# An Exp table loaded early, two converted matrices and one row maximum moved in the start of a three-stage attention kernel

## Chip, cores and metric

One NeuronCore of a Trainium2 chip runs the whole program. The metric is the device time of one execution in microseconds (us); the time shown for a kernel is the median of its runs.

## What is computed

Three stages follow each other for a batch of 4 with 576 positions. The first is decayed causal attention with 8 heads of 64, the second mixes the positions with a low-rank product and adds a feed-forward layer, the third is a mixture of four attention experts. The change touches only the first stage and the load of `U` and `V`, which the second stage starts with:

```python
log_f = np.log(np.clip(f, 0.0001, 1.0))
cum = np.cumsum(log_f, axis=-1)
scores = where(causal, -1e9, scale * q @ k.T + cum[:, :, :, None] - cum[:, :, None, :])
scores = scores - np.max(scores, axis=-1, keepdims=True)
attn = np.exp(scores); attn /= attn.sum(-1, keepdims=True) + 1e-9
x = attn @ v                      # first stage
h = x.transpose(0, 2, 1) @ U @ V  # start of the second stage
u = x + h.transpose(0, 2, 1)
```

## The kernel before

The first stage works through 32 heads in 16 pairs. For a head (0 is the first) the steps are these.

- `row_max` (lines 150 to 187) finds the maximum of each row of scores. It multiplies the queries by the keys into two PSUM tiles, `ua` (line 154, two products) and `ub` (line 163, four products), and VectorE adds the mask and reduces them: one instruction at line 158 for `ua`, four at line 176 for `ub`. TensorE then transposes the five columns of maxima (`mt`, line 181), VectorE scales them into `mr` (line 183), and two small DMAs on the SP queue (lines 185 and 186) put them into row 66 of the queries `qa`. `row_max` is a generator: `one(...)` runs it to its next `yield`. With `apart` true there is a stop between `ua` and `ub`.
- `scores` (lines 189 to 227) multiplies again, now with row 66 and with low parts, in two halves. The first half is a PSUM tile of five products, the second one of twelve (line 212). ScalarE takes the exponential of a half (line 221) and rounds it to float16 (`ph`, line 222); VectorE subtracts for the low part `pl` (line 223).
- `weighted_values`, `row_scales` and `normalise` multiply by the values and divide.

`ua`, `ub` and the score halves all come from one PSUM pool with two buffers (tag `s2` of pool `ps2`). A tile waits until what stood in its buffer has been read.

Before the first head, lines 446 to 458 take the logarithm of the decays on ScalarE (line 451), sum it and store it; `load_pair`, `split_high` and `split_low` (lines 482 to 522) load two heads, round them on ScalarE (lines 499 to 502), subtract on GpSimd (lines 519 to 522) and copy parts between partitions by DMAs on SP (lines 513 to 518).

`load_mix` (lines 584 to 599) loads `U` in one DMA and `V` in two (SP), as 64-bit words whose halves `narrow` (lines 302 to 310) makes into float32: a shift on VectorE (line 307), a scaled copy on ScalarE (line 308), and two more on VectorE (309, 310). For `U` three GpSimd copies follow (line 590), for each half of `V` a ScalarE copy and a GpSimd subtraction (lines 598, 599). The raw words share two buffers (tag `wraw`) and the results one (tag `wst`), so the second half of `V` can be loaded only when `U` is narrowed. `U` and `V` are first read by `mix(0)`, in head 3.

What sets the order. `first_batch` (lines 645 to 678) runs the first eight heads, and its TensorE instructions are issued in the order in which they are written. Everything before it, and the queues of VectorE, ScalarE, GpSimd and SP, are ordered by a planner that takes what it expects to be ready first. `tc.issue_after(ins)` makes the instructions of its block that go to `ins`'s queue stand behind `ins`; `cur["last"]` is the latest DMA of line 186, so in the kernel before the loads of `U` and `V` stand behind the row-maxima DMA of head 0, since line 630 comes before `first_batch`:

```python
    drain(maxima(0, 0))
    m_first = maxima(0, 1)
    one(m_first)               # head 1: ua and ub, ahead of first_batch
...
    with tc.issue_after(cur["last"].ins):
        load_mix()
```

In `first_batch` head `h` issues: first half of its scores, `ua` of head `h + 2`, second half of its scores, the transposed maxima of head `h + 1`, `ub` of head `h + 2`, and the weighted values of head `h - 1`. Between these stand the scales of the values and the mixing.

Of the kernel before, what the change touches and what calls it, by code (L numbers as in the profile page):

```python
# [8 lines left out]
F32 = mybir.dt.float32  # L9
# [4 lines left out]
AF = mybir.ActivationFunctionType  # L14
# [3 lines left out]
P = 128  # L18
# [35 lines left out]
def f32(ap):  # L54
    return ap.bitcast(F32)
# [3 lines left out]
def kernel(  # L59
# [13 lines left out]
    nc = tc.nc  # L73
# [4 lines left out]
    def pool(name, bufs=1, side="left", space=None):  # L78
        kw = {} if space is None else {"space": space}
        if space is None:  # L80
            kw["side"] = side
            kw["reuse_waits"] = "tile"
        return tc.alloc_tile_pool(name=name, bufs=bufs, **kw)
# [6 lines left out]
    small = pool("small", 4)  # L90
# [45 lines left out]
    cur = {}  # L136
# [5 lines left out]
    def drain(gen):  # L142

        while True:
            try:
                next(gen)
            except StopIteration as end:
                return end.value
# [80 lines left out]
    def weighted_values(ph, pl, vh, vl):  # L229

        av = ps1.tile([P, NT, 65], F32, name="av")
        for it in range(NT):
            order = list(range(it + 1)) if it < NT - 1 else [0, 4, 1, 2, 3]
            for jt in order:
                c = J_OFF[jt] + (it - jt) * P
                m = 64 if jt == 4 else P
                k = 64 if jt == 4 else P
                first, last = jt == order[0], jt == order[-1]
                nc.tensor.matmul(av[0:m, it, :], ph[0:k, c:c + m], vh[0:k, jt, :],  # L239
                                 start=first, stop=False)  # L240
                nc.tensor.matmul(av[0:m, it, 0:64], ph[0:k, c:c + m], vl[0:k, jt, :],  # L241
                                 start=False, stop=False)
                nc.tensor.matmul(av[0:m, it, :], pl[0:k, c:c + m], vh[0:k, jt, :],  # L243
                                 start=False, stop=last)
        return av
# [28 lines left out]
    def row_scales(av, rs, extra=None):  # L274

        den = small.tile([P, NT], F32, name="den")
        nc.vector.tensor_scalar(den[:], av[:, :, 64:65].rearrange("p t o -> p (t o)"),
                                1.0e-9 * PSCALE * VEXP, rs[:, 0:1], OP.add, OP.mult)
        rn = small.tile([P, NT], F32, name="rn")
        nc.vector.reciprocal(rn[:], den[:])  # L280
        if extra is not None:
            nc.vector.tensor_tensor(rn[:], rn[:], extra, OP.mult)
        return rn

    def normalise(dst, av, rn):
        nc.vector.tensor_tensor(dst, av[:, :, 0:64], rn[:].unsqueeze(2).to_broadcast([P, NT, D]),  # L286
                                OP.mult)
# [7 lines left out]
    def next_mx():  # L295
        counter[0] += 1
        return mxs[counter[0] % 4]
# [4 lines left out]
    def narrow(wt, raw, n, p0=0, p1=P):  # L302


        lo, hi = raw[p0:p1, :, 0], raw[p0:p1, :, 1]
        wi = wt.bitcast(I32)
        nc.vector.tensor_scalar(wi, lo, 29, None, OP.logical_shift_right)
        nc.scalar.activation(f32(lo), f32(hi), AF.Copy, scale=2.0 ** -112)
        nc.vector.scalar_tensor_tensor(wi, lo, 3, wi, OP.logical_shift_left, OP.bitwise_or)
        nc.vector.scalar_tensor_tensor(wi, hi, -2147483648, wi, OP.bitwise_and, OP.bitwise_or)  # L310
# [135 lines left out]
    fr = pre.tile([B * H, S], F32, name="fr")  # L446
# [2 lines left out]
    nc.vector.memset(ones[:], 1.0)  # L449
    nc.vector.tensor_scalar(fr[:], fr[:], 1.0e-4, 1.0, OP.max, OP.min)  # L450
    nc.scalar.activation(fr[:], fr[:], AF.Ln)
    cum = pre.tile([B * H, S], F32, name="cum")
    nc.vector.tensor_tensor_scan(cum[:], ones[:], fr[:], 0.0, OP.mult, OP.add)
    chl = pre.tile([B * H, 2, S], F32R, name="chl")
# [24 lines left out]
    def pair_heads(p):  # L479
        return heads[2 * (p % 2)], heads[2 * (p % 2) + 1]  # L480

    def load_pair(p):
        if p >= NPAIR:
            return
        sin = sins[p % 2 if p < NP else 0]
        qkt = sin.tile([P, 2, S], F32, name="qkt")
        nc.sync.dma_start(qkt[:], qk[p // NP, p % NP])
        vr = sin.tile([P, 2, NT, D], F32, name="vr")
        nc.sync.dma_start(vr[:], v[p // NP, p % NP])
        st_in[p] = (qkt, vr)  # L490
# [33 lines left out]
    def values(p):  # L524
        if p >= NPAIR:
            return
        vr = st_in[p][1]
        st_rs[p] = yield from value_scale(vr[:])
        value_parts(vr[:], st_rs[p], *vhs[p % 2])

    def maxima(p, j, apart=False):
        if p < NPAIR:
            yield from row_max(pair_heads(p)[j], next_mx(), apart)

    def one(gen):

        next(gen, None)

    def attend(p, j):
        vh, vl = vhs[p % 2]  # L540
        ph, pl = st_p[p, j]
        av = weighted_values(ph, pl, vh[:, j], vl[:, j])
        rn = row_scales(av, st_rs[p])
        normalise(xs[p][:, :, j * D:j * D + D], av, rn)
# [27 lines left out]
    split_low(0)  # L572
    drain(values(0))
    drain(maxima(0, 0))
    m_first = maxima(0, 1)
    one(m_first)
    load_pair(1)
    split_high(1)
    split_low(1)
# [4 lines left out]
    def load_mix():  # L584
        ur = stage.tile([P, 2 * NT * R], I32, name="ur", tag="wraw")
        nc.sync.dma_start(ur[:], u_in)
        u1 = stage.tile([P, NT * R], F32, name="u1", tag="wst", bufs=1)
        narrow(u1[:], ur[:].rearrange("p (n two) -> p n two", two=2), NT * R)
        for r in range(3):
            nc.gpsimd.tensor_copy(ut[:, :, r * R:r * R + R],  # L590
                                  u1[:].rearrange("p (t r) -> p t r", t=NT))
        for c in range(NC):
            cs = slice(c * HC, c * HC + HC)
            vraw = stage.tile([3 * R, 2 * HC], I32, name="vraw", tag="wraw")
            nc.sync.dma_start(vraw[:], v_in[:, 2 * c * HC:2 * c * HC + 2 * HC])
            vst = stage.tile([3 * R, HC], F32, name="vst", tag="wst", bufs=1)
            narrow(vst[:], vraw[:].rearrange("p (n two) -> p n two", two=2), HC, 0, 3 * R)
            nc.scalar.copy(vs[:, cs], vst[:])
            nc.gpsimd.tensor_tensor(vs[64:96, cs], vst[64:96, :], f32(vs[64:96, cs]), OP.subtract)
# [6 lines left out]
    def load_weights(wp, q):  # L606
        gen = load_quarter_steps(wp, q)
        W[q] = next(gen)
        behind.append(gen)
# [17 lines left out]

    load_weights(wx_pool, 0)
    load_weights(wy_pool, 1)
    with tc.issue_after(cur["last"].ins):  # L630
        load_mix()
    def weights_after(p):
        if p < len(WRATE):
            with tc.issue_after(cur["last"].ins):
                more_weights(WRATE[p])

    def next_inputs(p):
        load_pair(p)
        split_high(p)
        split_low(p)  # L640

    def pair_scores(p, j):
        st_p[p, j] = yield from scores(pair_heads(p)[j])

    def first_batch(m_next):

        mixing = vals = iter(())
        for h in range(2 * NP):  # L650
            p, j = divmod(h, 2)
            sc = pair_scores(p, j)
            m_last, m_next = m_next, maxima(p + 1, j, True)
            one(sc)
            one(m_next)
            if j == 0:
                xs[p] = sx.tile([P, NT, P], F32, name="x", bufs=2)
                vals = values(p + 1)
                one(vals)
            one(sc)  # L660
            one(m_last)
            if j == 1:
                next_inputs(p + 2)
            one(m_next)
            if j == 1:
                one(vals)
            if h > 0:
                attend(*divmod(h - 1, 2))
            if j == 0:
                one(vals)  # L670
                one(mixing)
            elif p > 0:
                mixing = mix(p - 1)
                one(mixing)
            if j == 1:
                weights_after(p)
        one(mixing)
        return m_next
# [64 lines left out]
    with tc.manual_schedule(engines={mybir.EngineType.PE}):  # L743
        later_batches(first_batch(m_first))
# [369 lines left out]
```

## Time and profile before

| | |
|---|---|
| median of 3 runs | 938.31 us (938.24 to 939.66) |
| span of the profiled execution | 939.0 us (the page gives no other time for it) |
| TensorE busy | 847.3 us, 90% |
| VectorE, ScalarE, GpSimd busy | 60%, 44%, 31% |
| mean granted TensorE clock | 0.954 |

The page's second part cuts the span into 40 slices of 23.5 us and gives the busy share of each engine in tenths, and under PEclk the granted clock of TensorE in tenths of full speed. The timeline gives each instruction with its start and its length; brackets show how long its engine had been idle and what ended that. The chain follows the work that ended last back to the start. SPq is the queue on which SP issues DMAs: its rows are the issue, not the transfer.

### The profile page before, as it was taken

The numbers are of one execution on the slowest core, as the hardware profiler recorded it, in microseconds if no ns is written. First come the engines' busy times: TensorE is split into PE (matmuls) and PEld (weight loads), VectorE is DVE, ScalarE is ACT, GpSimd is POOL, SyncE is SP. The second block draws the span as 40 slices with busy tenths as digits, with TensorE's granted clock in tenths as the row PEclk, the third lists the DMA queues.
The fourth block names the chain that finished last, engine by engine and source line by source line (L and its number), as shares of the span: only waits on it lengthen the run. The fifth ranks groups of instructions, "written<-read, shape, count | busy, mean of one in ns | idle before, by whom it ended". The sixth has DMA issues, their size and how long they took to land.

```text
span 939.0 us, 18998 instructions
## 1 busy us (share of the span) xinstructions
PE 847.3 (90%) x7480; PEld 792.6 (84%) x7480; DVE 562.3 (60%) x1468; ACT 415.3 (44%) x808; POOL 294.1 (31%) x262
## 2 busy tenths in 40 slices
PE   2886878999899989989998999999999897989897
PEld 2775767888899989989998999999999797978675
DVE  6798588787576657632256652222225778786653
ACT  4675546564445463332233342222113464644553
POOL 8545354353423333012135433323014131210100
PEclk9998567999999999999999999999999998989998
DMA  6345545353433341103178753424114130311222
GB/s 190 106 108 163 141 149 166 112 146 114 126 109 86 111 136 47 39 15 114 53 267 262 233 185 113 152 74 121 37 29 124 39 90 17 91 29 27 70 85 69
DMA packets 68777, 101.94 MB, mean 109 GB/s; under 512 B 6608, under 2 KB 49424, under 8 KB 68688
## 3 DMA queue, kind: packets, MB, share of 16 engines
q1 hardware_dynamic: 64416, 92.47, 33.4%
q10 hardware_dynamic: 4272, 8.26, 2.5%
q8 instruction: 59, 0.97, 0.4%
q14 instruction: 30, 0.25, 0.1%
HBM read 60.33 MB, written 22.56 MB: 88 GB/s over the span
## 4 chain that ended last, share of the span: by engine, by line
PE 70%; DVE 14%; DMA 6%; ACT 5%; issue 3%; POOL 1%; SPq 1%; POOLq 0%; ACTq 0%; DVEq 0%
PE cps L385 19%; PE hps L370 19%; PE sc L212 8%; PE pq L849 4%; PE po L935 3%; PE pv L892 3%; PE av L239 3%; DVE pl L223 2%; DMA ust<-udram 2%; PE ub L169 2%; DVE ub L176 2%; PE gp L552 2%; PE av L243 2%; PE av L241 2%; PE ua L156 1%
## 5 line engine op out<-in xcount | busy, mean ns | idle before, releaser
L385 PE MATMUL cps<-hh,w2h 128*128 128x288 f32 x512 | 155.4, 304 | 6.8 <-DVE yc L387 3.8
L223 DVE TENSOR_TENSOR pl<-pf,ph 128x576 f16<-128x576 f32 x144 | 121.6, 847 | 54.4 <-ACT ph L222 54.2
L385 PE MATMUL cps<-hh,w2l 128*128 128x288 f32 x512 | 152.2, 297 | 1.0 <-POOL w2l L345 1.0
L370 PE MATMUL hps<-uh,w1h 128*128 128x288 f32 x512 | 145.2, 305 | 6.7 <-ACT uh L355 6.7
L385 PE MATMUL cps<-hl,w2h 128*128 128x288 f32 x512 | 151.2, 295 | 0.0
L370 PE MATMUL hps<-uh,w1l 128*128 128x288 f32 x512 | 141.9, 299 | 0.0
L375 DVE SCALAR_TENSOR_TENSOR hl<-hps,hh 128x288 fp32r<-128x288 f32 x128 | 58.2, 455 | 127.3 <-ACT hh L374 127.1
L374 ACT ACTIVATE hh<-hps 128x288 fp32r<-128x288 f32 x128 | 52.3, 409 | 168.6 <-PE hps L370 168.4
L221 ACT ACTIVATE pf<-sc 128x576 f32<-128x576 f32 x144 | 83.6, 612 | 52.3 <-PE sc L212 48.6
L385 PEld LDWEIGHTS cps<-hh,w2h 128*128 128x128 f32 x512 | 97.1, 190 | 8.3 <-DVE yc L387 4.5
L370 PEld LDWEIGHTS hps<-uh,w1h 128*128 128x128 f32 x512 | 97.9, 191 | 7.2 <-ACT uh L355 7.2
L370 PEld LDWEIGHTS hps<-uh,w1l 128*128 128x128 f32 x512 | 98.0, 191 | 0.0
L385 PEld LDWEIGHTS cps<-hh,w2l 128*128 128x128 f32 x512 | 96.9, 189 | 1.2 <-POOL w2l L345 1.2
L385 PEld LDWEIGHTS cps<-hl,w2h 128*128 128x128 f32 x512 | 96.9, 189 | 0.0
L370 PE MATMUL hps<-ul,w1h 128*128 128x288 f32 x512 | 89.6, 297 | 3.2 <-POOL ul L356 3.2
L212 PE MATMUL sc<-qa,ka 67*128 67x288 f32 (+4 forms) x288 | 79.1, 334 | 14.6 <-DMA qa<-mr 5.5
L222 ACT CAST ph<-pf 128x576 f16<-128x576 f32 x144 | 88.7, 638 | 1.6
L239 PE MATMUL av<-vh,ph 128*128 128x65 f16 x720 | 86.4, 202 | 1.5 <-DVE x L286 1.5
L176 DVE CUSTOM_DVE_ANT_0 ub<-ub,maskm 128x448 f32<-128x448 f32 x192 | 81.4, 424 | 7.2 <-PE ub L169 6.0
L241 PE MATMUL av<-vl,ph 128*128 128x64 f16 x720 | 85.1, 198 | 0.0
L243 PE MATMUL av<-vh,pl 128*128 128x65 f16 x720 | 84.8, 198 | 0.0
L356 POOL TENSOR_TENSOR ul<-ust,uh 128x1152 fp32r<-128x1152 f32 x22 | 58.8, 2671 | 80.9 <-ACT uh L355 80.9
(160 smaller groups left out, 1984.9 us busy)
## 6 DMA issues: line engine op xcount, KB each, us to landing
raw<-in_w_dram SPq DMA_DIRECT2D x32, 512.0 KB
ust<-udram SPq DMA_DIRECT2D x22, 576.0 KB
qkt<-in_qk_dram SPq DMA_DIRECT2D x16, 576.0 KB
yc<-ydram SPq DMA_DIRECT2D x14, 576.0 KB
ydram<-yc SPq DMA_DIRECT2D x14, 576.0 KB
vr<-in_v_dram SPq DMA_DIRECT2D x16, 320.0 KB
udram<-ustage ACTq DMA_DIRECT2D x16, 288.0 KB
ydram<-ust SPq DMA_DIRECT2D x8, 576.0 KB
```

The source lines that it names most:

```text
L176: nc.vector.tensor_tensor_reduce(ub[0:n, bk, off:off + w], ub[0:n, bk, off:off + w], maskm[0:n, m0:m0 + w], 1.0, NEG, OP.add, OP.max, mx[0 ...
L212: nc.tensor.matmul(ps[:, bk, off:off + w], wa, xa, start=bk not in banks[:n], stop=bk not in banks[n + 1:])
L221: nc.scalar.activation(pfv, view, AF.Exp, scale=ISC)
L222: nc.scalar.copy(ph[:, o0:o0 + n], pf[:, 0:n])
L223: nc.vector.tensor_tensor(pl[:, o0:o0 + n], pf[:, 0:n], ph[:, o0:o0 + n], OP.subtract)
L239: nc.tensor.matmul(av[0:m, it, :], ph[0:k, c:c + m], vh[0:k, jt, :], start=first, stop=False)
L241: nc.tensor.matmul(av[0:m, it, 0:64], ph[0:k, c:c + m], vl[0:k, jt, :], start=False, stop=False)
L243: nc.tensor.matmul(av[0:m, it, :], pl[0:k, c:c + m], vh[0:k, jt, :], start=False, stop=last)
L356: nc.gpsimd.tensor_tensor(ul[:], ust[:], f32(uh[:]), OP.subtract)
L370: nc.tensor.matmul(ph[:], wa[:, k, fs], xa[:, k, :], start=n == 0, stop=n == 3 * KT - 1)
L375: nc.vector.scalar_tensor_tensor(hl[:], ph[:], 0.0, f32(hh[:]), OP.max, OP.subtract)
L385: nc.tensor.matmul(pc[:], wa[:, t, dsl], xa[:], start=n == 0, stop=n == 3 * FT - 1)
```

## The change

A one-row Exp on ScalarE stands behind the logarithm, so that the table of Exp is loaded there. The `ua` and `ub` products of head 1 leave the part ahead of `first_batch`: in head 0, `ua` now stands before the first half of the scores and `ub` behind it. `load_mix` moves into `first_batch` behind the DMAs of head 1's maxima.

```diff
     nc.scalar.activation(fr[:], fr[:], AF.Ln)
+    warm = small.tile([1, P], F32, name="warm", bufs=1)
+    nc.scalar.activation(warm[:], fr[0:1, 0:P], AF.Exp)
...
     drain(maxima(0, 0))
-    m_first = maxima(0, 1)
-    one(m_first)
+    m_first = maxima(0, 1, True)
     load_pair(1)
...
     load_weights(wy_pool, 1)
-    with tc.issue_after(cur["last"].ins):
-        load_mix()
+
     def weights_after(p):
...
             m_last, m_next = m_next, maxima(p + 1, j, True)
+            if h == 0:
+                one(m_last)
             one(sc)
+            if h == 0:
+                one(m_last)
             one(m_next)
...
             if h > 0:
                 attend(*divmod(h - 1, 2))
+            else:
+                with tc.issue_after(cur["last"].ins):
+                    load_mix()
             if j == 0:
```

## Rows read from the trace of the kernel before

**Rows 1.** The page: TensorE's granted clock by slice (part 2), the chain's shares (part 4).
```profile
PEclk9998567999999999999999999999999998989998
...
PE 70%; DVE 14%; DMA 6%; ACT 5%; issue 3%; POOL 1%; SPq 1%; POOLq 0%; ACTq 0%; DVEq 0%
```
**Rows 2.** The chain that ended last, first 120 us: start us, us, what.
```profile
17.75 0.68 SPq L186
18.48 2.32 DMA ur<-in_u_dram
20.82 0.64 DVE u L307
21.48 0.34 ACT ur L308
21.84 1.28 ACT L221
23.13 0.66 ACT pf L221
23.84 2.74 PE sc L212 x12
...
29.00 1.03 ACT ph L222 x2
30.05 1.44 PE sc L212 x5
```
**Rows 3.** The timeline of the start on ScalarE: start us, us, engine, line, operation.
```profile
3.54 0.68 ACT L451 ACTIVATE fr<-fr 32x576 f32<-32x576 f32 x1 [1.46 <-DVE fr L450]
...
6.00 0.67 ACT L499 CAST qa<-qkt 64x576 fp32r<-64x576 f32 x1 [1.77 <-DMA qkt<-in_qk_dram]
```
**Rows 4.** The same timeline where the maxima of heads 0 and 1 are reduced.
```profile
14.17 0.77 DVE L158 CUSTOM_DVE_ANT_0 ua<-ua,maskm 128x576 f32<-128x576 f32 x1 [0.54 <-PE ua L156]
...
15.24 0.59 SPq L518 DMA_DIRECT2D kb<-kb  x1
...
16.31 0.63 DVE L176 CUSTOM_DVE_ANT_0 ub<-ub,maskm 128x448 f32<-128x448 f32 x1 [0.68 <-PE ub L169]
...
16.86 0.27 DVE L183 TENSOR_SCALAR mr<-mt 5x128 fp32r<-5x128 f32 x1
...
17.16 0.55 SPq L185 DMA_DIRECT2D qa<-mr  x1
...
18.25 0.13 DVE L176 DVE_READ_ACCUMULATOR2_ANT mx<- 64x1 f32 x1
...
19.60 0.58 PE L212 MATMUL sc<-qa,ka 67*128 67x288 f32 x1 [3.11 <-DMA qa<-mr]
```
**Rows 5.** The same timeline: one low part, one `ub`, and head 3's reductions, first and last.
```profile
24.52 0.87 DVE L223 TENSOR_TENSOR pl<-pf,ph 128x576 f16<-128x576 f32 x1
...
26.44 1.20 PE L169 MATMUL ub<-ka,qa 66*128 66x448 f32 x4
...
45.63 0.63 DVE L176 CUSTOM_DVE_ANT_0 ub<-ub,maskm 128x448 f32<-128x448 f32 x1 [0.57 <-PE ub L169]
...
48.71 0.21 DVE L176 CUSTOM_DVE_ANT_0 ub<-ub,maskm 64x64 f32<-64x64 f32 x1
```
**Rows 6.** The same timeline: the second load of V, its two shifts, head 2's maxima.
```profile
23.87 0.33 SPq L595 DMA_DIRECT2D vraw<-in_vv_dram  x1
...
27.03 1.47 DVE L307 TENSOR_SCALAR vst<-vraw 96x288 int32<-96x288 int32 x1
...
33.89 0.30 DVE L307 TENSOR_SCALAR vst<-vraw 96x288 int32<-96x288 int32 x1
...
35.21 0.28 DVE L183 TENSOR_SCALAR mr<-mt 5x128 fp32r<-5x128 f32 x1
```
**Rows 7.** Windows of 5 us: length, busy us and count by engine, PEclk, DMA share, GB/s.
```profile
40.00:45.00 5.00, 4.85 (x22) 4.22 (x22) 2.24 (x6) 2.37 (x4) 2.73 (x3) 1.00 0.25 69
...
85.00:90.00 5.00, 0.00 (x0) 0.00 (x0) 5.00 (x7) 1.52 (x4) 4.84 (x3) 0.74 0.78 205
```

## The prediction

> **What bounds the kernel now.** I read the page first: the chain that ended last is on TensorE for 70% of the span, and the clock line shows four slices at 8, 5, 6 and 7 tenths behind the first three [rows 1]. The reader should see two regimes. Most of the span is matmul after matmul; what delays them all by a microsecond at the start delays the end by a microsecond. The first slices are not: there each head is a chain through TensorE, VectorE, ScalarE and the SP queue. So I read the chain of waits next, for the first 120 us. Between the maxima of head 0 leaving SP at 17.75 and its second score half at 23.84 it goes through the load of U, its shift, its scaled copy, a table load and the exponential [rows 2]. None of the first three belongs to head 0: ScalarE's queue has U's copy ahead of head 0's exponential. Then I read the timeline of the start, engine by engine, for what the moved instructions stand in front of [rows 3 to 6], and last the windows for where VectorE has room [rows 7].
>
> The sum is made against the profiled execution's span of 939.0 us. It lies 0.07% above the median of 938.31, and the page gives no other time for it; I carry differences over to the median unchanged.
>
> **The table load.** It costs 1.28 at 21.84 and the exponential follows at once [rows 2]. Moved, it starts when the logarithm ends, 3.54 + 0.68 = 4.22, and ends at 5.50. Behind it comes the new one-row Exp, which the trace of before does not have: 0.34 by U's copy of 160 elements, the nearest in length [rows 2], 0.68 by the logarithm at most [rows 3]. So ScalarE is free at 5.84 (6.18 at most), and its next work, a cast, starts at 6.00, when its data land [rows 3]. I take 0, with 0.18 as the upper end. What hides it is the wait for that load; without the cover it would cost 1.6. It issues no DMA.
>
> In these rows the load costs its own 1.28 and nothing more. The Trainium skill (ScalarE: Activation LUTs, What ACT_TABLE_LOAD costs) adds a drain of about 1.38 us to every switch, 2.66 in all. By that figure the casts would start about 1.2 us late, an estimate from the page; the gap of 0.01 us between load and exponential in rows 2 does not bear the drain out here.
>
> **Head 1's maxima, out of the way.** VectorE waits 0.54 for head 1's `ua` and then reduces it for 0.77, in the middle of head 0's own reductions; one reduction of head 1's `ub` (0.63) also begins before `mr` of head 0 at 16.86 [rows 4]. Without them `mr` comes near 16.86 - 0.54 - 0.77 - 0.63 = 14.9. But SP then still issues copies for pair 1, the last from 15.24 to 15.83 [rows 4], so line 185 is issued at about 15.85 instead of 17.16: 1.3 earlier. Ends: 0 if the planner leaves it where it is, 1.9 if it goes ahead of the last copy. Scores of head 0 then start at 19.60 - 1.30 = 18.3 [rows 4].
>
> **The first exponential.** Five products take 1.44 [rows 2], so the exponential can start at 19.75. Before it was 23.13: 3.4 us earlier, 1.3 of it from the maxima and 2.1 from U and the table.
>
> **Where this goes.** The change puts head 1's `ub` on TensorE behind that first half: 1.20 by rows 5, ending near 20.95. VectorE then reduces it. Before, the reductions stood in idle time ahead of the scores. The scores' second half needs a PSUM buffer, and there are two: one holds head 1's `ub`, the other `ua` of head 2. So what is late next is VectorE, not ScalarE. The four reductions ran from 16.31 to 18.38 in the start [rows 4], 2.1; from 45.63 to 48.9, 3.3, where other work was put between them [rows 5]. Low part `pl` of the first half, 0.87 [rows 5], becomes ready just then, and `ua` of head 2, 0.77 [rows 4], soon after. The buffer comes free at 23.05 with nothing between, 23.9 with `pl`, 24.7 with both. I take 23.9, since `pl` belongs to the earlier work and 3.3 lies between the ends too. Before, the second half started at 23.84 [rows 2]. The 3.4 us are given back: change +0.1, ends -0.8 and +0.9, and 0.6 less still if SP is early.
>
> From there the work is as before: twelve products, head 1's transposed maxima, `mr`, two DMAs, scores of head 1 at 30.05 [rows 2]. V's first shift of 1.47 [rows 6] and its scaled copy leave the space ahead of it. The chain puts that start down to the rounding `ph` that ended at 30.03 [rows 2], which stood behind V's copy. But those products read nothing of `ph`; they read row 66, and that lands 1.85 after line 186 in head 0 (17.75 to 19.60, rows 2, 4), whatever `ph` does. I count 0, with -0.6, V's copy and the pause ahead of it, as the lower end.
>
> **U and V.** Three DMA issues, about 0.33 each [rows 6], now stand on SP behind head 1's maxima. In head 0 this frees SP for pair 2's loads, which nobody waits for yet. Behind them stand pair 2's copies and head 2's maxima. The second load of V waits until U is narrowed, and SP with it; before, it was issued at 23.87, 3.05 after U had landed at 20.82 [rows 2, 6]. Now head 1's maxima leave SP near 30.05 - 1.85 = 28.2, U follows 0.68 later, lands 2.32 after that at 31.2 [rows 2], and the issue falls at 34.2. Head 2's `mr` starts at 35.21 [rows 6], so I take 0, with 1 us as the upper end. VectorE gets U's three steps (at most 3.05 less the copy's 0.34, 2.7) and half of V in head 1, where it had V's other half before, whose shift took 0.30 there [rows 6]. What is left falls into 40 to 45, where VectorE is busy only 2.24 of 5 us [rows 7]; that hides it. The copies of U and subtractions of V on GpSimd move along. The reader of both is head 3's mixing, so nobody waits. I count 0; without the cover the price is the narrowing itself, as in V's rival below.
>
> **Sum:** 0 (table) + 0.1 (head 0) + 0 (head 1) + 0 (U, V), less 0.2, a third of the lower end, for `ph` in head 1: -0.1. Forecast 938.2 us, no change that can be told; about 0.2%, 1.9 us, is what a measurement of this kernel can tell. The ends together would be -2.0 and +2.1; its own range is the most of that, 936.5 to 940.2.
>
> **Rivals.**
>
> *The gain is kept* (faster). If the reductions do not decide, the second half follows `ub` (1.20) and `ua` (two products, some 0.8 of the 1.44 that five take) on TensorE: 21.75, 2.1 earlier than 23.84. With the lower end of head 1, 0.6, it is 2.7. All behind it moves with it: 935.6. For it: VectorE is through with head 1 at 18.4 and has nothing urgent once U is gone. Against it: two buffers, and both are emptied by VectorE. Chance 0.24.
>
> *The clock* (faster). TensorE does nothing from 85 to 90 us [rows 7], and behind this its clock line shows 5 and 6 tenths, the 1.2 GHz level for most of two slices, 47 us [rows 1]. If VectorE's order there changes and TensorE keeps 2.4 GHz, the 70% of these that the chain spends on it, 33 us, halve at best: 16. Other engines then take over the chain; I take half, 8: 930.3. A shorter slow stretch gives less. For it: VectorE and GpSimd are both full there, so order matters. Against: nothing of the change stands there. Chance 0.12. The other sign, a slow stretch longer by one slice, would cost a quarter of a slice's 23.5 by the same reckoning, up to 6; I take 4: 942.3, chance 0.08.
>
> *V ahead of head 2's maxima* (slower). If the planner puts a half of V in front of `mr` of head 2 on VectorE, `mr` waits for the shift at its long price 1.47 [rows 6], ScalarE's copy (0.34 by U's, rows 2) and one more VectorE step (0.30 to 0.64, rows 2, 6): 2.3. It decides once the shift starts later than 35.2 - 2.3 = 32.9. For it: both want that place. Against: before, V's other half stood there at 0.30 and cost little. 940.6, chance 0.18.
>
> *The table in the way.* If a switch had a cost behind the load as long as the load itself, 1.28 [rows 2], ScalarE would be free at 5.84 + 1.28 = 7.1, the casts 1.1 late, SP's first copies with them, and all of head 0: 939.4. The exponential directly behind the load speaks against it [rows 2]. The page of the Trainium skill named above is the rule behind this case. Chance 0.02.
>
> **How the numbers follow.** No change holds 0.36 for the forecast and 0.02 for the table: 0.38. Faster: 0.24 + 0.12 = 0.36. Slower: 0.18 + 0.08 = 0.26. The range takes in the kept gain and V's rival with the ends of the unknown costs, and leaves out most of both clock cases: 933.5 to 942.3.
>
> **What would show it.** Right: one table load ending near 5.5 and casts still at 6.0; line 185 at about 15.9; the first exponential near 19.8; the second half of head 0 waiting for VectorE's line 176, not for ScalarE, and starting near 24; head 1's scores near 30; no wait of `mr` of head 2 on V. Wrong: the second half of head 0 starting by 22.5 and head 1's scores by 28; `mr` of head 2 a microsecond or more away from 35.2; or a clock line that differs in the slices that now show 5 to 8.

## The result and the profile after

| | before | after |
|---|---|---|
| median | 938.98 us (938.24 to 940.8, 4 runs) | 947.38 us (945.17 to 950.72, 4 runs) |
| profiled execution | span 939.0 us, clock 0.954 | 950.72 us, span 949.0 us, clock 0.944 |
| TensorE busy | 847.3 us | 852.7 us |

The ratio is 1.008 with a 95% interval of 1.0051 to 1.0109: the changed kernel is slower by 0.8%, some 7.5 us, and outside the predicted range. Of all runs reported here one, of e4_after_q4, was in the chip's slower state; it counts in that kernel's median and not in its ratio.

The page of the changed kernel, clock line and shares of the chain; they answer to [rows 1].

```profile
PEclk9978568999899999999999999999999898999999
...
PE 69%; DVE 12%; DMA 10%; ACT 4%; issue 2%; POOL 2%; SPq 1%; POOLq 0%; ACTq 0%; DVEq 0%
```

DMA has 10% of the chain where it had 6%, and the third slice (47 to 71 us) shows a dip that was not there before. First the start, on the timeline of the changed kernel (start us, us, engine, line, operation); these lines answer to [rows 2 to 4].

```profile
4.23 1.28 ACT L453 ACT_TABLE_LOAD   x1
5.53 0.31 ACT L453 ACTIVATE warm<-fr 1x128 f32<-1x128 f32 x1
5.74 0.65 ACT L501 CAST qa<-qkt 64x576 fp32r<-64x576 f32 x1
...
13.90 0.77 DVE L158 CUSTOM_DVE_ANT_0 ua<-ua,maskm 128x576 f32<-128x576 f32 x1 [0.46 <-PE ua L156]
...
14.99 0.59 SPq L520 DMA_DIRECT2D kb<-kb  x1
...
15.83 0.28 DVE L183 TENSOR_SCALAR mr<-mt 5x128 fp32r<-5x128 f32 x1 [0.47 <-PE mt L181]
16.13 0.56 SPq L185 DMA_DIRECT2D qa<-mr  x1
...
18.57 0.58 PE L212 MATMUL sc<-qa,ka 67*128 67x288 f32 x1 [2.78 <-DMA qa<-mr]
...
20.04 0.65 ACT L221 ACTIVATE pf<-sc 128x576 f32<-128x576 f32 x1 [8.02 <-PE sc L212]
...
21.55 1.73 DVE L223 TENSOR_TENSOR pl<-pf,ph 128x576 f16<-128x576 f32 x1
23.20 0.75 DVE L158 CUSTOM_DVE_ANT_0 ua<-ua,maskm 128x576 f32<-128x576 f32 x1
...
24.07 1.22 PE L212 MATMUL sc<-qa,ka 67*128 67x320 f32 x3 [2.47 <-DVE mx L158]
...
29.98 0.58 PE L212 MATMUL sc<-qa,ka 67*128 67x288 f32 x1 [1.89 <-DMA qa<-mr]
```

The table is loaded behind the logarithm, head 0's maxima leave SP at 16.13 instead of 17.16, the first exponential starts at 20.04 instead of 23.13, the second half at 24.07 instead of 23.84. Head 1's scores stand at 29.98 (before 30.05). So far nothing is won and nothing lost. Now the same timeline from 34 to 50 us, beside [rows 5, 6].

```profile
34.54 0.33 SPq L596 DMA_DIRECT2D vraw<-in_vv_dram  x1
...
35.15 0.28 DVE L183 TENSOR_SCALAR mr<-mt 5x128 fp32r<-5x128 f32 x1 [0.69 <-PE mt L181]
...
36.63 0.47 DVE L307 TENSOR_SCALAR vst<-vraw 96x288 int32<-96x288 int32 x1
...
39.37 1.61 DVE L309 SCALAR_TENSOR_TENSOR vst<-vraw,vst 96x288 int32<-96x288 int32 x1
...
41.18 0.44 DVE L310 SCALAR_TENSOR_TENSOR vst<-vraw,vst 96x288 int32<-96x288 int32 x1
...
43.77 0.35 SPq L489 DMA_DIRECT2D qkt<-in_qk_dram  x1
...
44.80 0.55 SPq L185 DMA_DIRECT2D qa<-mr  x1
...
45.74 0.29 DVE L307 TENSOR_SCALAR vst<-vraw 96x288 int32<-96x288 int32 x1
...
49.10 0.58 PE L212 MATMUL sc<-qa,ka 67*128 67x288 f32 x1 [2.06 <-DMA qa<-mr]
```

V's first half is narrowed from 36.63 to 41.6, in the middle of head 2's and head 3's reductions, and its second half begins at 45.74. On SP the 576 KB load of pair 4 (line 489) now stands ahead of the two small DMAs of head 3's maxima. Before, the planner had it behind them: those at 45.22 and 45.82, the load at 47.19. TensorE pauses 2.06 us ahead of head 3's scores; the longest pause before, between 36 and 52 us, was 0.66.

Windows of the kernel before (length, then busy us and count of TensorE, weight loads, VectorE, ScalarE and GpSimd, granted clock, DMA share, GB/s):

```profile
44.00:60.00 16.00, 14.23 (x191) 12.78 (x191) 13.51 (x43) 11.70 (x21) 7.92 (x6) 1.00 0.40 107
```

And of the changed kernel:

```profile
44.00:60.00 16.00, 13.20 (x132) 11.94 (x130) 10.76 (x37) 8.80 (x17) 6.68 (x6) 0.63 0.32 86
```

From 44 to 60 us TensorE is busy nearly as long but has 132 matmuls in the records instead of 191 (part of that is other work, since the heads come later): the granted clock is 0.63, which is the 1.2 GHz level for most of the window, where it was 1.00. As an estimate, the lost clock is worth at most 13.20 x (1 - 0.63) = 4.9 us of TensorE's work. The first exponentials of the heads, from the same timelines (us), show when it is paid:

| head | 0 | 1 | 2 | 3 | 4 | 5 | 7 | 8 | 15 |
|---|---|---|---|---|---|---|---|---|---|
| before | 23.1 | 31.5 | 41.1 | 48.5 | 56.4 | 63.3 | 77.6 | 94.5 | 196.9 |
| after | 20.0 | 31.4 | 40.7 | 50.6 | 61.0 | 67.7 | 82.1 | 99.1 | 204.1 |

Head 3 is 2.1 us later than before and head 4 4.6; nothing more is lost up to head 8, and 2.6 more by head 15. Behind that the two kernels run side by side until the last part, where the profiled execution of the changed one loses 3 more.

### The profile page after: what moved, and what is told of

Its sections match the earlier page's. It is cut to its first block, busy times and chain, and to the rows that moved or that the text cites. A ratio compares the mean times of both kernels' runs of the same rounds, so it can differ in the third digit from the quotient of the medians.

```text
span 949.0 us, 19009 instructions
## 1 busy us (share of the span) xinstructions
PE 852.7 (90%) x7480; PEld 798.5 (84%) x7480; DVE 560.4 (59%) x1468; ACT 415.2 (44%) x809; POOL 291.3 (31%) x262
## 4 chain that ended last, share of the span: by engine, by line
PE 69%; DVE 12%; DMA 10%; ACT 4%; issue 2%; POOL 2%; SPq 1%; POOLq 0%; ACTq 0%; DVEq 0%
PE hps L370 18%; PE cps L385 17%; PE sc L212 10%; PE pq L856 4%; DMA ust<-udram 4%; PE pv L899 3%; PE po L942 3%; PE av L239 2%; DVE pl L223 2%; PE ub L169 2%; PE gp L554 2%; DMA qa<-mr 2%; DVE ub L176 2%; PE av L243 2%; PE av L241 2%
## 5 line engine op out<-in xcount | busy, mean ns | idle before, releaser
L375 DVE SCALAR_TENSOR_TENSOR hl<-hps,hh 128x288 fp32r<-128x288 f32 x128 | 58.2, 455 | 128.2 <-ACT hh L374 128.0
L370 PEld LDWEIGHTS hps<-uh,w1h 128*128 128x128 f32 x512 | 98.0, 191 | 10.5 <-ACT uh L355 10.4
L239 PE MATMUL av<-vh,ph 128*128 128x65 f16 x720 | 88.4, 204 | 1.5 <-DVE x L286 1.5
L176 DVE CUSTOM_DVE_ANT_0 ub<-ub,maskm 128x448 f32<-128x448 f32 x192 | 81.5, 424 | 11.4 <-PE ub L169 10.5
L241 PE MATMUL av<-vl,ph 128*128 128x64 f16 x720 | 87.0, 200 | 0.0
L243 PE MATMUL av<-vh,pl 128*128 128x65 f16 x720 | 86.7, 200 | 0.0
```

The lines of the kernel that those rows point to most:

```text
L176: nc.vector.tensor_tensor_reduce(ub[0:n, bk, off:off + w], ub[0:n, bk, off:off + w], maskm[0:n, m0:m0 + w], 1.0, NEG, OP.add, OP.max, mx[0 ...
L370: nc.tensor.matmul(ph[:], wa[:, k, fs], xa[:, k, :], start=n == 0, stop=n == 3 * KT - 1)
L375: nc.vector.scalar_tensor_tensor(hl[:], ph[:], 0.0, f32(hh[:]), OP.max, OP.subtract)
```

## The experiments

Three theories were held against each other, and the expectations use their letters.

- **A**, the place of the load: pair 4's 576 KB ahead of head 3's maxima on SP is what costs.
- **B**, V: its six VectorE steps in heads 2 and 3 delay these heads.
- **C**, the clock: whatever delays them, the time is paid at TensorE's lower level. To follow it I counted, in windows of 1 us from 44 to 300 us of each profiled execution, those with a granted clock under 0.8. I call them low us; the kernel before has 63, the changed one 77.

Each run is compared with the kernel before on its own chip; the ratio and its interval are the recorded ones and can lie 0.2% off the quotient of the medians. All runs without spare products in one table; "maxima late" means head 1's maxima inside head 0, "V late" the loads of U and V behind head 1's maxima, "ahead" and "behind" the place of pair 4's load against head 3's maxima. The last two columns give the us between the first exponentials of heads 3 and 4, and of heads 11 and 12. They and the low us are read from one profiled execution each, while the ratio is from all runs; that of e3 was the second slowest of its ten (947.37 us).

| run | maxima | V | load | median us | ratio (95%) | low us | heads 3 to 4 | heads 11 to 12 |
|---|---|---|---|---|---|---|---|---|
| before | early | early | behind | | 1 | 63 | 7.9 | 18.3 |
| e1_table (with table) | early | early | behind | 939.06 | 0.9986 (0.9957 to 1.0014) | 56 | 7.7 | 18.2 |
| e7_before_q4 | early | early | ahead | 946.78 | 1.0057 (1.0027 to 1.0087) | 69 | 9.8 | 16.8 |
| e2_mix | early | late | ahead | 945.76 | 1.0051 (1.0025 to 1.0077) | 76 | 10.0 | 11.8 |
| e11_mix_load_behind | early | late | behind | 936.25 | 0.9958 (0.993 to 0.9986) | 48 | 9.7 | 10.4 |
| e13_table_mix_load_behind (with table) | early | late | behind | 934.77 | 0.9948 (0.9921 to 0.9974) | 52 | 9.1 | 10.7 |
| e3_max | late | early | ahead | 941.84 | 1.0012 (0.9981 to 1.0043) | 64 | 10.0 | 20.3 |
| e8_no_mix (with table) | late | early | ahead | 943.75 | 1.0053 (1.0018 to 1.0087) | 67 | 11.8 | 20.3 |
| e9_no_mix_load_behind (with table) | late | early | behind | 944.58 | 1.0058 (1.0026 to 1.0089) | 68 | 10.9 | 20.4 |
| after (with table) | late | late | ahead | 947.38 | 1.008 (1.0051 to 1.0109) | 77 | 10.5 | 16.0 |
| e4_after_q4 (with table) | late | late | behind | 948.37 | 1.0074 (1.0048 to 1.01) | 81 | 13.4 | 13.6 |
| e12_no_v (with table) | late | not narrowed | ahead | 941.73 | 1.0012 (0.9984 to 1.0041) | 64 | 6.8 | 19.9 |
| e10_no_v_load_behind (with table) | late | not narrowed | behind | 933.41 | 0.9936 (0.9905 to 0.9966) | 60 | 11.4 | 10.3 |

### Each part of the change alone

The table alone:

```diff
     nc.scalar.activation(fr[:], fr[:], AF.Ln)
+    warm = small.tile([1, P], F32, name="warm", bufs=1)
+    nc.scalar.activation(warm[:], fr[0:1, 0:P], AF.Exp)
```

> Only the table load moves; the order of SP's queue around head 2 stays as in the kernel before (the maxima DMA of head 3 ahead of the 576 KB load of pair 4). Theory A (that load ahead of the maxima makes head 3 late and the clock falls) and theory B (U and V narrowed in heads 1 to 3 hold up VectorE and ScalarE) both expect no loss: first exponential at 21.8, head 3's first exponential at 47.3 to 48.6, 936.5 to 939.5 us.

The move of U and V alone:

```diff
-    with tc.issue_after(cur["last"].ins):
-        load_mix()
...
             if h > 0:
                 attend(*divmod(h - 1, 2))
+            else:
+                with tc.issue_after(cur["last"].ins):
+                    load_mix()
```

> Only U and V move. Here the load of pair 4 stands ahead of head 3's maxima on SP as in the changed kernel. Theory A: head 3's first exponential at 50 or later, a stretch at 1.2 GHz between 48 and 60 us, 943 to 948. Theory B expects the same time, 943 to 948, but with the wait on VectorE's or ScalarE's narrowing, not on the maxima's DMA.

Head 1's maxima alone:

```diff
-    m_first = maxima(0, 1)
-    one(m_first)
+    m_first = maxima(0, 1, True)
...
+            if h == 0:
+                one(m_last)
             one(sc)
+            if h == 0:
+                one(m_last)
             one(m_next)
```

> Only head 1's maxima move; U and V are narrowed as early as in the kernel before. The load of pair 4 stands ahead of head 3's maxima on SP here too. Theory A: head 3 late by about 2, then clock, 943 to 948. Theory B: no loss, 936 to 940.

Alone, the three are worth -0.14%, +0.51% and +0.12%; together they should make +0.5%, and the change has +0.8%. Only U and V differ from no change. In that run heads 1 and 2 come earlier (first exponentials at 30.0 and 37.7 instead of 31.5 and 41.1), so the move does what it is for, and then heads 3 and 4 are late or level (48.2 and 58.2). In this run and in that of the maxima the planner had also put pair 4's load ahead of head 3's maxima, so the parts alone don't tell the theories apart.

### The load's place

The changed kernel with pair 4's load held behind those DMAs:

```diff
+    lasts = {}
...
     def next_inputs(p):
-        load_pair(p)
+        if p == 4:
+            with tc.issue_after(lasts[3].ins):
+                load_pair(p)
+        else:
+            load_pair(p)
...
             one(sc)
             one(m_last)
+            lasts[h + 1] = cur["last"]
```

> The changed kernel with one order forced: the load of pair 4's queries and keys behind head 3's maxima on SP. Theory A: the maxima land about 1.9 after their issue instead of 3.7, head 3's first exponential near 48.5, no 1.2 GHz stretch at 49 to 58, about 4.5 us back: 939 to 943. Theory B: head 3's first exponential stays at 50.5, 945 to 950.

And the other way round, the kernel before with that one load (its queries and keys) ahead, nothing else (`load_qk` is the part of `load_pair` that loads them):

```diff
...
             one(sc)
-            one(m_last)
+            if h == 2:
+                early[4] = load_qk(4)
+                with tc.issue_after(cur["qk"].ins):
+                    one(m_last)
+            else:
+                one(m_last)
```

> The kernel before with the load of pair 4's queries and keys forced ahead of head 3's maxima on SP, nothing else. Theory A: the maxima land 1.9 us later, head 3's first exponential at 50 instead of 48.5, head 4's at 59 to 61, 943 to 946. Theory C: the same if the wait lowers the clock in heads 3 and 4; if the clock stays up, only about 1.5 later, 940 to 942. Theory B: 938 to 941.

The load alone is enough to make the kernel before 0.57% slower; its head 4 starts at 60.9 instead of 56.4. Its timeline:

```profile
45.65 0.54 SPq L486 DMA_DIRECT2D qkt<-in_qk_dram  x1
46.28 0.55 SPq L185 DMA_DIRECT2D qa<-mr  x1
...
50.27 0.37 PE L212 MATMUL sc<-qa,ka 67*128 67x288 f32 x1 [1.30 <-DMA qa<-mr]
```

From the issue of line 185 to head 3's scores it is 3.99 us. In the kernel before, where the load stands behind, it is 47.66 - 45.22 = 2.44 (the same timeline):

```profile
45.22 0.55 SPq L185 DMA_DIRECT2D qa<-mr  x1
...
47.66 0.37 PE L212 MATMUL sc<-qa,ka 67*128 67x288 f32 x1
```

But with the load behind, the changed kernel stays where it was, 1.0074, although its head 3 starts at 49.2 instead of 50.6. Another pause has taken the place of the first:

```profile
50.15 0.67 DVE L223 TENSOR_TENSOR pl<-pf,ph 128x512 f16<-128x512 f32 x1
50.81 0.43 DVE L309 SCALAR_TENSOR_TENSOR vst<-vraw,vst 96x288 int32<-96x288 int32 x1
...
51.58 0.21 DVE L176 CUSTOM_DVE_ANT_0 ub<-ub,maskm 64x64 f32<-64x64 f32 x1
...
51.90 1.22 PE L212 MATMUL sc<-qa,ka 67*128 67x320 f32 x3 [1.51 <-DVE ar L257]
```

The second half of head 3 starts when VectorE has done the last reduction of `ub` at 51.8, and a step of V stands ahead of it. So the load's place (A) is sufficient in one kernel and not the whole cause in the other.

### Spare products against the clock

Products into a PSUM tile that is written over afterwards: 8 ahead of each first half in heads 1 to 7, 40 ahead of the mixing behind head 7, 30 ahead of the first product of the feed-forward layer; in the kernel before and in the changed one.

```diff
+    def spin(dst, n):
+        for _ in range(n):
+            nc.tensor.matmul(dst, identb[:], maskm[:, 0:HC], start=True, stop=True)
...
+            if u == 0:
+                spin(ps[:, 0, 0:HC], cur.get("hold", 0))
```

> The kernel before with spare products whose result is overwritten: 8 ahead of the first half of the scores in heads 1 to 7, 40 ahead of the mixing behind head 7, 30 ahead of the first feed-forward product. They fill TensorE's longest waits up to 125 us. On SP the load of pair 4 happens to stand ahead of head 3's maxima here. Theory C (what the change costs is TensorE's clock): no low stretch from 48 to 120 us, 925 to 934 us. Theory A (that load's place): head 3 late, 940 to 946.

> The changed kernel with the same spare products; on SP the load of pair 4 stands behind head 3's maxima here. Theory C: the low stretches of heads 3, 4, 7 and behind go, and the time comes within 3 us of the kernel before with spare products, 925 to 935. Theory A: faster than that kernel by 4 or more, 936 to 941. Theory B (the narrowing of U and V holds up VectorE and ScalarE): slower than that kernel by 6 or more.

The kernel before became slower with them, 947.83 us (1.0055, 1.0023 to 1.0086), the changed one stayed at 947.6 (1.0076, 1.0054 to 1.0099). The low us fell to 58 and 35, yet the time did not follow. The spare products are work of their own, and in the first of the two pair 4's load went ahead of the maxima as well. The pair is inconclusive; it proves C neither right nor wrong.

### V, the maxima and the load

The changed kernel with U and V loaded where they were, once as it comes and once with the load held behind:

```diff
     load_weights(wy_pool, 1)
+    with tc.issue_after(cur["last"].ins):
+        load_mix()
...
-            else:
-                with tc.issue_after(cur["last"].ins):
-                    load_mix()
```

> The changed kernel with the loads of U and V put back where they were (behind head 0's maxima); table and head 1's maxima as changed. Pair 4's load stands ahead of head 3's maxima, as in the changed kernel. Theory A (the place of that load alone costs some 5 us): 943 to 946 us, ratio 1.003 to 1.006, head 4's first exponential past 59 us. Theory B (V's steps in heads 2 and 3 are what costs): no V there any more, so 937 to 941, ratio 0.997 to 1.001, head 4's first exponential near 57. Theory C (what counts is the time that TensorE spends at 1.2 GHz between 44 and 300 us, 63 us in the kernel before and 77 in the changed one, whatever takes it there): no value of its own, but the difference in time from the kernel before is about half the difference in these low us.

> As the run with U and V put back, and pair 4's load held behind head 3's maxima. Theories A and B both: 936 to 940 us, ratio 0.995 to 1.001, head 3's first exponential near 48 and head 4's near 56. If it is slower than 1.003, neither the load's place nor V's steps is the cause, and head 1's maxima are, with the order of VectorE that they bring.

Both are slow, 1.0053 and 1.0058. Against what both theories expected of the second one, U and V in their old place don't heal the changed kernel (0.2 to 0.3% better, with intervals that overlap), and the load's place makes no difference. What is left in it against the run with the table alone is the move of head 1's maxima, from 0.9986 to 1.0058 (head 4 at 61.3 instead of 57.1). That part was costed at a gain. V's six steps end at 35.9 us in this run, so it is not they that stand among the reductions of head 3 here.

Next V's narrowing left out of the changed kernel, with the load held behind and as it comes. Of the computation it leaves out the values of V: zeros stand in their place.

```diff
-            narrow(vst[:], vraw[:].rearrange("p (n two) -> p n two", two=2), HC, 0, 3 * R)
+            nc.gpsimd.memset(vst[:], 0.0)
```

> The changed kernel with pair 4's load held behind head 3's maxima, and with the narrowing of both halves of V left out (three VectorE instructions and one of ScalarE each; zeros are put in its place by GpSimd, so the mixing multiplies by zeros; loads, ScalarE's copy and GpSimd's subtraction stay). Beside the changed kernel with that load held behind (948.37 us, ratio 1.0074) it differs by V's narrowing alone. Theory B: head 4's first exponential near 57 instead of 62.6 and ratio 0.997 to 1.002. Theory A or head 1's maxima as the cause: no change, ratio 1.005 or more. Theory C: whichever it is, half of the difference in low us.

> The changed kernel as it is, pair 4's load ahead of head 3's maxima, with V's narrowing left out (as in the run with that load behind: zeros take its place, so the mixing multiplies by zeros; the loads, ScalarE's copies and GpSimd's subtractions stay). Theory A (in the changed kernel the load's place is what costs): 943 to 948 us, ratio 1.003 to 1.008, a pause of TensorE of 2 us or so ahead of head 3's scores. Theory B (V's steps together with the moved maxima): as with the load behind, 931 to 937 us, ratio 0.990 to 0.998, although the pause for the load stays. In both, the time follows the low us of the clock between 44 and 300.

Without V's steps the changed kernel falls from 1.008 to 1.0012 with the load ahead, and from 1.0074 to 0.9936 with it behind. So the changed kernel's loss needs V's narrowing, as B has it: with the load ahead head 4 comes at 56.2 instead of 61.0, and most of the 0.7% is there. The run with the load ahead is slower than B expected and faster than A did. The edit takes out two scaled copies on ScalarE with the six steps on VectorE and puts zeros into the mixing; no run parts these, and none takes U's narrowing out.

The windows of the two, the load ahead first and then behind, beside those of the two kernels above:

```profile
44.00:60.00 16.00, 14.65 (x195) 12.97 (x193) 13.38 (x45) 12.22 (x23) 8.48 (x7) 1.00 0.39 107
...
44.00:60.00 16.00, 14.43 (x110) 12.35 (x107) 11.54 (x39) 8.90 (x17) 7.73 (x6) 0.60 0.39 106
```

In the first the clock is 1.00 again with 195 matmuls, as in the kernel before, and the pause ahead of head 3's scores is 0.72 although the load still stands ahead. In the second the clock is as low as in the changed kernel, head 4 comes at 58.4, and yet it is the fastest kernel of the table. So its 0.8% over the first is not the wait of head 3's maxima for the load, and a low clock from 44 to 60 us does not settle the time; where the 0.8% comes from is shown below.

Last the move of U and V without the move of the maxima, with the load held behind, and the same with the table:

> The kernel before with the move of U and V alone (945.76 us, ratio 1.0051, when it was run with pair 4's load ahead of head 3's maxima), and that load held behind them. Theory A: the loss goes, ratio 0.996 to 1.001, head 4's first exponential near 54, as early as its head 2 (37.7, 3.4 us earlier than in the kernel before) allows. Theory B: V's steps still delay heads 3 and 4, ratio 1.003 to 1.006, head 4 past 57.

> The kernel before with the table loaded early, the move of U and V, and pair 4's load held behind head 3's maxima; head 1's maxima stay ahead of the first batch. If the moved maxima are the part that harms: as the same without the table or a little better, 932 to 938 us, ratio 0.992 to 0.998, under 56 low us between 44 and 300. If any new order of the queues can bring the clock down: 940 or more, with 65 low us or more.

The edit of the second against the kernel before (the first is without the two lines of `warm`; `lasts` is filled as shown above):

```diff
+    warm = small.tile([1, P], F32, name="warm", bufs=1)
+    nc.scalar.activation(warm[:], fr[0:1, 0:P], AF.Exp)
...
-    with tc.issue_after(cur["last"].ins):
-        load_mix()
...
+        if p == 4:
+            with tc.issue_after(lasts[3].ins):
+                load_pair(p)
...
+            else:
+                with tc.issue_after(cur["last"].ins):
+                    load_mix()
```

Both beat the kernel before, by 0.42% and 0.52%, and the second beats the changed kernel by some 12 us. The windows of the second, and behind them the last stretch in the kernel before:

```profile
44.00:60.00 16.00, 14.47 (x152) 12.85 (x151) 14.01 (x44) 10.22 (x20) 7.77 (x6) 0.89 0.39 106
...
140.00:200.00 60.00, 58.38 (x575) 52.95 (x573) 52.85 (x147) 39.34 (x75) 29.11 (x20) 1.00 0.50 145
...
140.00:200.00 60.00, 54.04 (x487) 49.06 (x488) 48.70 (x128) 34.63 (x66) 26.96 (x18) 0.89 0.45 135
```

The clock dips in head 3 here too (0.89), but from 140 to 200 us it stays at 1.00, where the kernel before has 0.89 and issues 487 matmuls instead of 575. The start of the second run, on the timeline:

```profile
21.50 0.65 ACT L221 ACTIVATE pf<-sc 128x576 f32<-128x576 f32 x1 [8.01 <-PE sc L212]
22.20 1.22 PE L212 MATMUL sc<-qa,ka 67*128 67x320 f32 x3 [0.15 <-ACT pf L221]
```

The first exponential is 1.6 us earlier than before and the second half follows it at once, at 22.20; it waits for no reduction. But that lead does not last: head 3 starts at 48.4 (before 48.5) and head 4 at 57.5, 1.1 us later than before. What makes this kernel faster opens between heads 11 and 12, 10.7 us apart instead of 18.3. There the kernel before waits for weights of the feed-forward layer, which ScalarE rounds (line 344); this is its timeline:

```profile
147.94 0.62 ACT L344 CAST w2h<-wst 128x512 fp32r<-128x512 f32 x1
...
148.61 0.40 PE L385 MATMUL cps<-hh,w2h 128*128 128x288 f32 x1 [2.01 <-ACT w2h L344]
...
150.03 0.61 PE L385 MATMUL cps<-hh,w2l 128*128 128x288 f32 x1 [1.02 <-POOL w2l L345]
```

And that of the second run:

```profile
146.61 0.62 ACT L344 CAST w2h<-wst 128x512 fp32r<-128x512 f32 x1
...
148.98 0.29 PE L385 MATMUL cps<-hh,w2h 128*128 128x288 f32 x1
```

Here the rounding is done before TensorE asks for it. In the kernel before ten low us follow the wait (149 to 158), in this run none. The other two kernels that beat the kernel before, e11 and e10, have no wait there either. So what the three gain opens there and not in the first heads: they are 1.8 to 3.3 us later than the kernel before at head 11 and 4.6 to 6.1 us earlier at head 12. Between e10 and e12 it is the same, 4.3 us later at head 11 and 5.3 earlier at head 12. None of this is a price of V, of the maxima or of the load in heads 0 to 4, and no run tests that wait by itself.

### What the table of runs says together

Two rules describe it. The slower kernels (1.005 and over) are those with the load ahead (e7, e2) and those with head 1's maxima late while V is narrowed (e8, e9, e4, after); the ones at or under 1 have neither (before, e1, e11, e13, e10). In the second group the load's place changes nothing (e8 and e9, after and e4). Two runs stand between, at 1.0012: the load ahead without V, and the maxima alone (e3). The second does not fit well: it differs from e8 by the table only, and e8 is at 1.0053; their intervals overlap, so the two may be one value.

The stretch from head 3 to head 4 shows what the rules have in common. It takes 6.8 to 7.9 us in the three kernels without a low us between 44 and 60 (before, e1, e12) and 9.1 to 13.4 in the ten others, which have 4 to 13 of them there. So each of the three things that harm, the load ahead in the kernel before, the late maxima, and V's steps with them, makes this stretch longer, and they don't add up: by head 4 the changed kernel is 4.6 us late, and the load alone makes it 4.5.

The low us go with the time: over the 13 kernels of the table the correlation of ratio and low us is 0.88 and the straight line through them has 0.42 us of time for each low us. A us at half speed loses half a us of work at most, so the line is about what C asks for. It is not the whole account: the fastest kernel, e10, has 60 low us, 3 fewer than the kernel before, and is 0.6% faster. The mean granted clock of all runs of the changed kernel has a median of 0.9495, against 0.953 to 0.9545 for the kernel before on the other chips, and within one kernel 0.01 of clock goes with mostly some 3 to 6 us; by that the clock carries 1 to 3 of the 7.5 us. The two runs with the table, V in its old place and the maxima late (e8, e9) have 0.955 and 0.952, hardly lower than before, and still lose 5. How the loss divides between the pauses themselves and the clock behind them stays open; the spare products could not part the two.

## Why the prediction was wrong

**Right up to head 2.** The table load ends at 5.51 and costs nothing, as reckoned; alone it is worth -0.14%, an interval that holds 0. The Exp follows the load by 0.02 us, and the cast starts at 5.74, even before its old time. The Trainium skill (ScalarE: Activation LUTs, What ACT_TABLE_LOAD costs) adds a drain of about 1.38 us to each switch; by that the cast would have started about 1.1 us late, an estimate from the page, and the trace does not bear it out. Line 185 came at 16.13 (predicted 15.85), the scores at 18.57 (18.3), the first exponential at 20.04 (19.75), the second half at 24.07 (23.9), head 1's scores at 29.98 (30), the second load of V at 34.54 (34.2), `mr` of head 2 at 35.15 (35.2). The time of line 185 was luck. I had `mr` near 14.9 and SP busy with copies until 15.83. But only `ub` of head 1 left VectorE's way: its `ua` is still reduced ahead, at 13.90, `mr` came at 15.83, and SP had been free since 15.58. The 3.4 us (3.1 measured) were given back to VectorE, as forecast. One detail was off there: the half waited for the reduction of head 2's `ua` (line 158), which stood behind a `pl` that took 1.73 and not 0.87; three of the four reductions of head 1's `ub` came later still, until 25.8.

**The step that failed: the two zeros behind head 0, "From there the work is as before" and, for U and V, "I count 0", because "nobody waits".** Head 4 of the changed kernel starts 4.6 us later than before, and V's narrowing is needed for that: without it head 4 is in time (56.2, before 56.4) and the ratio is 1.0012 instead of 1.008. I looked for who reads V, and found only head 3's mixing. But V's six steps stand on VectorE's queue among the reductions and low parts of heads 2 and 3, for which TensorE waits. The room that was to hide them, 2.24 of 5 us busy from 40 to 45 [rows 7], is not where they fell: V's first half ran from 36.63 to 41.6, where VectorE had been busy for 3.75 of 4 us before (36 to 40), and the window itself was then nearly full. It is shown for the changed kernel and for the one without V's steps:

```profile
40.00:45.00 5.00, 4.28 (x26) 3.94 (x26) 4.29 (x12) 3.22 (x6) 4.43 (x4) 0.71 0.33 84
...
40.00:45.00 5.00, 4.85 (x21) 4.27 (x22) 1.88 (x5) 2.21 (x4) 3.02 (x5) 1.00 0.26 75
```

Without its cover V was to cost at most the narrowing itself, 2.3 us; it measured 0.7%, some 6 us, 4.8 of them by head 4: from 44 to 60 us the changed kernel has 12 low us, and none without V's steps. The 1.4% of the pair with the load behind is not that price alone, since e10 gains between heads 11 and 12 as well. V's place is not the whole of it: with the maxima late, V early still loses (e8, 1.0053), and with the maxima early, V late stays within 1 us of the kernel before (e11: head 4 at 57.4 against 56.4, head 8 at 94.0 against 94.5). Which pause takes the clock down in heads 3 and 4 stays open.

**The part that was credited.** The maxima of head 1 were costed by what head 0 gains from their leaving: 1.3 us predicted, 1.0 measured (line 185 at 16.13 instead of 17.16). That was about right for head 0, and so was "given back"; there the account was closed. With V narrowed early the move alone goes from 0.9986 to 1.0058 (e1 and e9), and the loss opens in head 4, where its reductions are long past. That they had filled idle time of VectorE before the first scores, and now stand in the chain of heads, fits head 0; how it reaches head 4 is not shown.

**What was not seen.** SP's queue was followed as far as head 2's maxima. "In head 0 this frees SP for pair 2's loads, which nobody waits for yet" stops too early: the planner moved pair 4's load in front of head 3's maxima, and by itself that costs the kernel before 0.57%. Nor does a microsecond at the start simply reach the end, as the prediction's first paragraph has it: e13 leads by 1.6 us at head 0, is 1.1 behind at head 4, and is 0.5% faster in the end.

**The clock's slower case** had the right sign and the wrong place. I looked at the slow slices that were there [rows 1] and wrote that nothing of the change stands there. A new slow stretch opened in heads 3 and 4, where the clock had been at 1.00. With a chance of 0.08 and 4 us it was too rare and too cheap: the stretch from 44 to 60 us alone is worth up to 4.9 us by the estimate above. V's rival, 940.6 us, named the right work; but it put the price on one `mr` of head 2, which came in time.

## What to carry to other kernels

An idle stretch on an engine can be spent only once: when a change moves several things into it, or moves one and takes away the work ahead of another, cost the pieces together and on the engine's queue, not by who reads the result. Where a planner orders the queues, read the changed order of every queue, a few heads past the edit, for large loads that have come ahead of small transfers on which TensorE waits; hold them with an explicit order. And before a cause is named, follow the granted clock and the heads over the whole trace: here a low stretch opened in ten of thirteen kernels where the kernel before had none, and the gains of the fastest three opened at a wait 100 us behind the edit.

## What the runs showed of the hardware

- The place of one 576 KB load on the queue made the two small DMAs behind it (0.2 and 2 KB) land later. From the issue of line 185 to head 3's scores it is 3.30 to 4.30 us in the six kernels of the table with the load ahead, and 2.44 to 2.98 in the seven with it behind. The price is shown by itself in one pair alone, 0.57% in the kernel before (e7); the pair of e2 and e11 differs by 0.9%, but only 0.7 us of that stand there at head 4.
- The granted clock of a window is 1.00 up to 42 us in both kernels although the matmuls run at two speeds there: a product of 288 columns of the scores took 0.44 us in head 2 of the kernel before (at 39.99) and 0.30 in that of the changed one (at 40.01). The changed kernel had reached the faster one earlier, and fell to a granted 0.52 in the window from 42 to 44 us; the kernel before reached it near 46 us and kept it to 87. Why the earlier rise was followed by a fall no run here shows. A long pause is not always ahead of one: with the maxima late and V early (e8) the longest pause between 38 and 52 us was 0.74, and the clock fell near 52.
- Steps of the same size took very different times on VectorE: line 309 on 96x288 took 1.61 us at 39.37 in the changed kernel and 0.43 at 50.81 in the run with the load behind. In the first, GpSimd ran line 271 from 39.21 to 40.67; in the second it did nothing from 49 to 53.
